# GraphSAGE sampling and aggregation on one Trainium2 core: merging the third part beside the second's decode, closing the first counts behind sort stages, counting on VectorE, key transfers from GpSimd, quarter broadcasts

## The chip, the core and the metric

One core of one Trainium2 chip runs the whole program. The metric is device microseconds of one execution; the number that counts is the median of three runs. The core's engines run side by side, each through its own queue of instructions in order: TensorE (PE, with its weight loads PEld), VectorE (DVE), ScalarE (ACT), GpSimd (POOL) and SyncE (SP). They wait for each other, and for transfers, by semaphores. SyncE, ScalarE and GpSimd issue transfers. Here semaphores named DMAHW count transfers that SyncE or ScalarE issued, those named DMASW the transfers of GpSimd; there are eight of each and they are used in turn.

## The reference, cut to what matters

```python
N, deg, D = 12500, 64, 64
E = N * deg                                   # 800,000 edges, src and dst drawn at random
nsum = _segment_sum(x[src], dst, N)           # for every edge: nsum[dst] += x[src]
h_neigh = nsum * deg_inv[:, None]
return x @ w_self + h_neigh @ w_neigh
```

## The kernel before

**Sort.** Every edge becomes one key that holds a bucket number and the two indices inside it: `dst` is cut in 87 blocks of 144, `src` in 98 blocks of 128, so there are 87 x 98 = 8,526 buckets of about 94 edges. 128 rows of 6,250 keys are sorted side by side, by stages of VectorE that take the minimum and maximum at a distance (`sort_runs`, L220). The last 30 stages (APART) are cut in portions, low columns first, so that the low part of the rows is final before the high part.

**Parts.** The buckets fall in three parts, numbered 0 to 2 in the code and called part 1, 2 and 3 in the text: 32, 20 and 16 buckets in each of 128 rows. For each part, `find_rows` counts on ScalarE, row by row, where each of its 128 stretches begins (L448, 128 counts); `st` (L451, VectorE), a transpose (TensorE) and `ix` (L455, VectorE) make indices of the counts; `gather_runs` lets GpSimd gather 128 runs by them (L463, one indirect transfer each, with one small memset as a pause behind it, or two behind the first 32 of part 1). `merge_runs` merges the 128 sorted runs on VectorE pair by pair (L276, L288), in groups (GROUPS) that are merged as their runs arrive. Then `find_buckets` or `find_and_gather` counts in windows of the merged rows where each bucket begins (L608), `store_rows` writes the rows to memory, `gather_window` gathers each bucket (L627), and `decode_buckets` splits the keys into the source and the destination index inside the bucket: `split` on VectorE (L677, L679), `narrow` on ScalarE (L684 to L690; the source indices go to memory as `sl`), `turn` on TensorE and ScalarE (L696, L697; the destination indices stay in SBUF as `dlT`). What lies beyond a bucket's place goes through `leftovers`: a list `top` is written to memory (`tops`), read back as `many`, reduced by VectorE (`ltop`, L741), written again (`lt`) and read again (`lk`). In the kernel before ScalarE issues these four transfers.

**The tile phase.** Eight buckets make a tile; there are 1,069. For 28 buckets (a chunk, 3.5 tiles) SyncE broadcasts the `sl` rows to all partitions (`slb`, L796, three buffers), and VectorE makes one-hot matrices from them (`ohs`, L798) and from `dlT` (`ohd`, L801). A tile then is 8 matmuls that pick the source rows (`ct`, L826), one eviction by ScalarE (`xg`, L836) and 16 matmuls that add them to the destinations (`acc`, L880). VectorE builds one-hots 44 buckets ahead.

**What sets the order.** From `after_sort` on the order is written by hand. `sums_and_merge` runs a loop over the tiles and places the other work between them. Part 1 is merged and decoded before the loop. In the loop, `change` goes through part 2 and then part 3: the merges first, at a rate of PACE nanoseconds of estimated VectorE time a tile, then the search and gather of buckets, then the decode. The gathers of part 3's runs are placed at one for two tiles, all in GpSimd's queue, where they wait for no tile. Once `self.changed` is set, VectorE takes a share of the evictions (L834).

Replaying the loop gives the tiles at which the work stands before: merges of part 2 to tile 247, its search and decode to 327, merges of part 3 to 656, its search and decode to 727, then 342 tiles with nothing beside them.

Of the kernel before, what the change touches and what calls it, by code (L numbers as in the profile page):

```python
# [40 lines left out]
GROUPS = ((32, 32, 32, 32), (64, 32, 32), (128,))  # L41
FIRST = 96
FROM_TILE = (0, 60, 0)
PACE = (0, 500, 420)
# [80 lines left out]
NC1 = len(WIN.w1)  # L125


def constants():
# [5 lines left out]
    for p in range(NP):  # L134
# [3 lines left out]
        first = np.array([lo + n / 2 + 0.25 for lo, n in WIN.w2[p]])  # L138
# [121 lines left out]
def merge_round(nc, src, oth, off, rstride, nruns, ln, lout, late):  # L260
# [6 lines left out]
    def at(t, first, n, step=1):  # L267
        return view(t, off + first, [[2 * ln, n2], [step, n]])
# [63 lines left out]
class Kernel:  # L332
# [136 lines left out]
    def merge_runs(self, part, u, pong):  # L469
# [8 lines left out]
        def round_(level, off, rstride, nruns):  # L478
            src = bufs[par[level]]
            args = nc, src, bufs[1 - par[level]], off, rstride  # L480
            if part == 0 and level == 6:
                def done(rows):
                    self.rows, self.lower = rows, True
                yield from merge_last(*args, lens[level], lens[level + 1], LOWER, done)
            else:
                yield from merge_round(*args, nruns, lens[level], lens[level + 1], lambda: self.late)
# [3 lines left out]
        for n in GROUPS[part]:  # L490
            level, rs, nr = 0, lens[0], n
            while nr > 1:
                yield from round_(level, first * lens[0], rs, nr)
                rs, nr, level = 2 * lens[level], nr // 2, level + 1
# [4 lines left out]
            while len(done) > 1 and done[-1][0] == done[-2][0]:  # L499
                (level, f1), (_, f0) = done.pop(), done.pop()  # L500
                yield from round_(level, f0 * lens[0], (f1 - f0) * lens[0], 2)
                done.append((level + 1, f0))
        self.rows = bufs[par[-1]]

    def store_rows(self, part, queue):
        queue.dma_start(self.d2[part][:, SIDE:SIDE + LROW[part]], self.rows[:, :LROW[part]])
# [92 lines left out]
    def junk(self):  # L599
        return self.keep.tile([128, max([512] + [n for ws in WIN.w2 for _, n in ws])], BF, name="junk2")  # L600

    def count_below(self, part, k, acc):
# [4 lines left out]
        w = view(self.rows, lo, [[1, n]])  # L607
        nc.scalar.activation(self.junk()[:, :n], w, AF.Sign, bias=c2[:, 2, k:k + 1], accum_out=acc[:, k:k + 1])  # L608

    def find_buckets(self, part):  # L610
# [4 lines left out]
        nc.sync.dma_start(self.d2[part][:, SIDE:SIDE + LOWER], self.rows[:, :LOWER])  # L615
        for k in range(KPRS[part]):
            if k == NLOWER:
                nc.sync.dma_start(self.d2[part][:, SIDE + LOWER:SIDE + LROW[part]], self.rows[:, LOWER:LROW[part]])
# [23 lines left out]
    def find_and_gather(self, part, vp):  # L642
# [6 lines left out]
        ix = self.keep.tile([128, kpr], U32, name=f"ix2_{part}")  # L649
        for k in range(kpr + LAG):  # L650
            if k == 1:
                self.store_rows(part, nc.scalar)
            if k < kpr:
                self.count_below(part, k, acc)
            if k >= LAG:
                g = k - LAG
                nc.scalar.activation(ix[:, g:g + 1], acc[:, g:g + 1], AF.Relu, scale=-0.5, bias=self.c2[part][:, 3, g:g + 1])  # L657
# [3 lines left out]
    def decode_buckets(self, part, v, vp, mps):  # L661
# [10 lines left out]
        def split(k, n, vk, _):  # L672
            w = vp.tile([128, 4, 128], I32, name="w", bufs=4 if part else 2)[:, :n]
# [8 lines left out]
        def narrow(k, n, vk, w):  # L682
            c = c0 + k // 4
            nc.scalar.activation(self.junk()[:, :n * 128], w.rearrange("p k s -> p (k s)"), AF.Sign, bias=self.edge[:, :1], accum_out=self.cnt[:, c:c + 1])  # L684
            l16 = vp.tile([128, 4, 128], BF, name="l16", bufs=4)
# [3 lines left out]
            l16 = vp.tile([128, 4, 128], BF, name="l16", bufs=4)  # L689
# [16 lines left out]
        e = self.rows if part else vp.tile([128, kpr * 2 * EXT], F32, name="e")  # L706
# [36 lines left out]
    def leftovers(self, part):  # L743
# [5 lines left out]
        nc.scalar.dma_start(self.tops[part], self.top.rearrange("p j i -> p (j i)"))  # L749
# [484 lines left out]
```

## Time and profile before

| | us |
|---|---|
| median of 3 runs (lowest, highest) | 2102.41 (2098.67, 2104.05) |
| the profiled execution's own time | 2093.24 |
| its span in the profile | 2091.5 |
| busy in the span: DVE, ACT, PE, POOL | 1869.5, 1440.1, 1060.4, 822.5 |
| sort, counts, part 1 up to the first tile | 0 to 911.8 |
| tile phase | 911.8 to 2076 |

The profile is one execution. Busy time is a mean over stages with different limits, so the stage tables are read first: for each stretch of time the busy microseconds of each engine. In the groups, a row reads: line, engine, operation, output and inputs with their shape, count, busy microseconds, mean nanoseconds of one, idle time of the engine ahead of them and what ended it. In the waits, a row reads: who waited for whom, microseconds in total, times, the longest. In the timeline, a row reads: start, duration, engine, line, operation. In the chain, a row reads: start, duration, what.

### The profile page before, as it was taken

The numbers are of one execution on the slowest core, as the hardware profiler recorded it, in microseconds if no ns is written. First come the engines' busy times: TensorE is split into PE (matmuls) and PEld (weight loads), VectorE is DVE, ScalarE is ACT, GpSimd is POOL, SyncE is SP. The second block draws the span as 40 slices with busy tenths as digits, with TensorE's granted clock in tenths as the row PEclk, the third lists the DMA queues.
The fourth block names the chain that finished last, engine by engine and source line by source line (L and its number), as shares of the span: only waits on it lengthen the run. The fifth ranks groups of instructions, "written<-read, shape, count | busy, mean of one in ns | idle before, by whom it ended". The sixth has DMA issues, their size and how long they took to land.

```text
span 2091.5 us, 60398 instructions
## 1 busy us (share of the span) xinstructions
PE 1060.4 (51%) x26074; PEld 913.7 (44%) x26074; DVE 1869.5 (89%) x2127; ACT 1440.1 (69%) x2455; POOL 822.5 (39%) x1003
## 2 busy tenths in 40 slices
PE   0060000000000000048888877889989878989987
PEld 0050000000000000047777766777877767878876
DVE  8999999299999998999999957999999858888985
ACT  7470005707884005358889999999989998888986
POOL 1000000198889850999999955101020131101101
PEclk9999999999999999998999999899999999999998
DMA  4271000001100000256677786677687867868874
GB/s 152 51 162 23 0 5 12 18 13 58 20 19 12 14 10 33 67 198 238 241 241 249 245 280 221 214 266 261 246 270 254 298 220 236 290 252 288 276 287 133
DMA packets 126816, 333.17 MB, mean 159 GB/s; under 512 B 70996, under 2 KB 82508, under 8 KB 126284
## 3 DMA queue, kind: packets, MB, share of 16 engines
q1 hardware_dynamic: 90212, 306.28, 41.0%
q0 software_dynamic: 32032, 20.73, 7.1%
q8 instruction: 205, 3.36, 0.6%
q10 hardware_dynamic: 4296, 2.22, 0.4%
q14 instruction: 71, 0.58, 0.1%
HBM read 306.31 MB, written 22.85 MB: 157 GB/s over the span
## 4 chain that ended last, share of the span: by engine, by line
DVE 47%; PE 22%; ACT 13%; issue 9%; POOL 6%; DMA 2%; ACTq 0%; DVEq 0%; SPq 0%; POOLq 0%
DVE u L288 15%; PE ct L826 13%; PE acc L880 8%; DVE b L220 7%; DVE ohd L801 6%; DVE a L220 6%; DVE ohs L798 5%; ACT xg L836 5%; POOL u L463 5%; DVE u L276 3%; ACT junka L448 2%; ACT junk L608 2%; DVE u L320 1%; ACT u L272 1%; DMA slb<-sl 1%
## 5 line engine op out<-in xcount | busy, mean ns | idle before, releaser
L836 ACT ACTIVATE xg<-ct 128x1024 f16<-128x1024 f32 x1017 | 968.5, 1101 | 90.1 <-PE ct L826 70.1
L463 POOL DMA_INDIRECT u<-d,ix x384 | 512.2, 1334 | 424.3 <-ACT junka L448 360.6
L826 PE MATMUL ct<-xh,ohs 128*128 128x128 f16 x8526 | 622.7, 226 | 73.9 <-ACT xg L836 37.9
L826 PEld LDWEIGHTS <-ohs 128*128 128x128 f16 x8526 | 515.9, 101 | 123.6 <-issue 55.3
L288 DVE TENSOR_TENSOR u<-u 128x496 f32<-128x496 f32 (+46 forms) x664 | 491.2, 772 | 24.3 <-ACT u L272 15.0
L880 PE MATMUL acc<-ohd,xg 64*128 64x72 f16 x17052 | 424.1, 197 | 82.5 <-ACT xg L836 51.4
L798 DVE TENSOR_SCALAR ohs<-slb,pidx 128x3584 f16<-128x3584 bf16 x305 | 352.9, 1157 | 69.9 <-PE ct L826 64.4
L880 PEld LDWEIGHTS <-xg 64*128 64x128 f16 x17052 | 334.8, 96 | 162.9 <-ACT xg L836 61.4
L801 DVE TENSOR_TENSOR ohd<-iota,dlT 128x2016 f16<-128x2016 bf16 x305 | 365.7, 1199 | 0.0
L453 PE MATMUL stp<-idf,st 128*128 128x128 f32 x3 | 1.4, 465 | 504.2 <-DVE st L451 504.2
L952 POOL DMA_DIRECT2D out<-o x26 | 45.1, 1755 | 538.2 <-ACT o L946 521.1
L448 ACT ACTIVATE junka<-b,c 128x220 bf16<-128x220 f32 (+43 forms) x384 | 171.2, 446 | 100.4 <-DVE b L220 89.3
L453 PEld LDWEIGHTS stp<-idf,st 128*128 128x128 f32 x3 | 0.5, 182 | 505.1 <-DVE st L451 256.5
L220 DVE TENSOR_TENSOR b<-a 128x918 f32<-128x918 f32 (+50 forms) x184 | 214.7, 1214 | 4.8 <-ACT a L222 0.3
L220 DVE TENSOR_TENSOR a<-b 128x918 f32<-128x918 f32 (+47 forms) x170 | 198.3, 1210 | 4.5 <-ACT b L222 2.0
L272 ACT ACTIVATE u<-u 128x512 f32<-128x512 f32 (+15 forms) x129 | 56.6, 504 | 156.0 <-DVE u L276 155.9
L627 POOL DMA_INDIRECT v<-d,ix x68 | 87.6, 1289 | 162.5 <-ACT ix L657 81.4
L696 PE MATMUL tr<-idb,l 128*128 128x128 bf16 x68 | 8.4, 261 | 233.5 <-ACT l L690 233.5
L222 ACT ACTIVATE a<-b 128x1 f32<-128x1 f32 (+44 forms) x57 | 23.4, 426 | 137.6 <-DVE b L220 134.6
L696 PEld LDWEIGHTS <-l 128*128 128x128 bf16 x68 | 4.8, 113 | 236.2 <-ACT l L690 235.7
L378 POOL MEMSET pad<- 128x89 f32 x448 | 103.2, 230 | 2.0
L834 DVE CAST xg<-ct 128x1024 f16<-128x1024 f32 x52 | 63.5, 1223 | 43.8 <-PE ct L826 40.0
(130 smaller groups left out, 831.2 us busy)
## 6 DMA issues: line engine op xcount, KB each, us to landing
slb<-sl SPq DMA_DIRECT2D x305, 896.0 KB
u<-d,ix POOLq DMA_INDIRECT x384
xt<-xh SPq DMA_DIRECT2D x1, 3136.0 KB
own<-os SPq DMA_DIRECT2D x12, 256.0 KB
out<-os SPq DMA_DIRECT2D x12, 256.0 KB
out<-o POOLq DMA_DIRECT2D x24, 126.0 KB
rd<-dst SPq DMA_DIRECT2D x4, 521.0 KB
rs<-src SPq DMA_DIRECT2D x4, 521.0 KB
```

What stands on the lines that cost most here:

```text
L220: nc.vector.tensor_tensor(view(dst, lo + sh, [[st, g], [1, l]]), x, y, op=op)
L272: nc.scalar.activation(at(src, a, e - a), at(oth, a, e - a), AF.Copy)
L288: nc.vector.tensor_tensor(to, at(cur, ln + lo, n), at(cur, lo + k, n), op=op)
L378: self.nc.gpsimd.memset(self.pad, 0.0)
L448: nc.scalar.activation(junk[:, :n], w, AF.Sign, bias=self.c1[:, 0, c:c + 1], accum_out=a)
L463: nc.gpsimd.indirect_dma_start(out=u[:nr, p * w:(p + 1) * w], out_offset=None, in_=src, in_offset=bass.IndirectOffsetOnAxis(ap=self.start[ ...
L627: self.nc.gpsimd.indirect_dma_start(out=self.v[:, k].bitcast(F32), out_offset=None, in_=flat(self.d2[part], 128 * PITCH2[part]), in_offset ...
L798: nc.vector.tensor_scalar(s.rearrange("p c s -> p (c s)"), b, self.pidx[:, :1], None, op0=OP.is_equal)
L801: nc.vector.tensor_tensor(d, self.iota[:, None].to_broadcast([128, 14, HN, 2]), ix, op=OP.is_equal)
L826: nc.tensor.matmul(ct[:, i * 128:(i + 1) * 128], cols[i][0], self.xh[:, (b0 + i) % NB].rearrange("p a f -> p (a f)"), start=True, stop=True)
L836: nc.scalar.activation(xg[:, :cnt * 128], ct[:, :cnt * 128], AF.Copy)
L880: nc.tensor.matmul(acc[h][:, db % OCT * HN:(db % OCT + 1) * HN], xg[r, i * 128:(i + 1) * 128], d[r], start=db % OCT == 0 and sb == 0, stop ...
```

## The change

**First counts (part 1).** The 64 counts that were left behind the first portion of the sort are placed among the first 24 stages of the second portion (BEFORE = 24); `st`, the transpose, `ix` and the gathers come behind its 25th stage; five stages and the last portion follow.

```diff
-            for _ in rows:
-                pass
...
-            for _ in self.gather_runs(0, u0):
-                pass
-            for step in portions[1]:
+            for i, step in enumerate(portions[1]):
                 step()
+                while i < BEFORE and next(rows) + 1 < EARLY + (128 - EARLY) * (i + 1) // BEFORE:
+                    pass
+                if i == BEFORE:
+                    for _ in rows:
+                        pass
+                    rows = None
+                    for _ in self.gather_runs(0, u0):
+                        pass
```

On VectorE, where `a` and `b` are the two sort buffers, `st_930`/`ix_934` and `st_992`/`ix_996` are part 1's in the kernel before and in the changed one. Before:

```order
L220 TENSOR_TENSOR b<-a 128x797 x2
L451 TENSOR_TENSOR st_930<-c_116,acc_741 128x128
L455 SCALAR_TENSOR_TENSOR ix_934<-stp,prow_117 128x128
L220 TENSOR_TENSOR a<-b 128x18x53 x2
L220 TENSOR_TENSOR b<-a 128x23x41 x2
```

After:

```order
L223 TENSOR_TENSOR a<-b 128x306x3 x2
L454 TENSOR_TENSOR st_992<-c_116,acc_741 128x128
L458 SCALAR_TENSOR_TENSOR ix_996<-stp,prow_117 128x128
L223 TENSOR_TENSOR b<-a 128x459x2 x2
L223 TENSOR_TENSOR a<-b 128x459x2 x2
```

`st` moved from behind the first portion's last stage (797 pairs) to behind the second portion's 25th.

**Third part beside the second's decode.** `change` no longer holds the merges. Two strands run in the loop: `merge` (parts 2 and 3, at PACE 450 a tile, where it was 500 and 420) and `chain` (search, gather and decode of a part that is merged). Part 3's merges begin when part 2's end; its 128 runs are merged in two groups of 64, each begun when its gathers have been placed 8 tiles before. The second merge buffer of part 3 is half as large, `w` and `l16` have two buffers in place of four, and `self.changed` is set where part 3's merges end, not its decode.

```diff
-GROUPS = ((32, 32, 32, 32), (64, 32, 32), (128,))
+GROUPS = ((32, 32, 32, 32), (64, 32, 32), (64, 64))
-FROM_TILE = (0, 60, 0)
-PACE = (0, 500, 420)
+FROM_TILE = 50
+BEFORE = 24
+PACE = 450
...
+            if chain:
+                if last != "gather" or not n % 2 and self.picked < n - 1:
+                    last = next(chain, None)
...
+            t += PACE
+            while t > 0 and merge:
+                if merging == 1 and n < FROM_TILE and self.grouped[1] >= FIRST:
+                    t = 0
+                elif merging == 2 and self.grouped[2] < 128 and (
+                        len(gathered) < self.grouped[2] + 64 or n < gathered[self.grouped[2] + 63] + 8):
+                    t = 0
+                else:
+                    dt = next(merge, None)
```

Replaying the changed loop: merges of part 2 to tile 270, its search and decode from 270 to 356, merges of part 3 from 270 to 616, its search and decode to 684, then 385 tiles.

**Later counts by VectorE.** For parts 2 and 3, `count_below` becomes one VectorE instruction that compares and sums; the constants hold the window's start in place of its middle, and the index is made on ScalarE without the factor -0.5.

```diff
+        if part:
+            nc.vector.tensor_scalar(junk[:, :n], w, c2[:, 1, k:k + 1], None, op0=OP.is_lt, op1=OP.add,
+                                    accum_out=acc[:, k:k + 1])
+        else:
+            nc.scalar.activation(self.junk[:, :n], w, AF.Sign, bias=c2[:, 2, k:k + 1], accum_out=acc[:, k:k + 1])
```

On VectorE, while part 2 is searched and decoded (`u` and `u_2108` are part 3's two merge buffers in the changed kernel, `acc_1` part 2's counts). Before, at the start of part 2's decode:

```order
L801 TENSOR_TENSOR ohd<-iota,dlT 128x2016
L708 MEMSET top_12088 128x72
L677 SCALAR_TENSOR_TENSOR w<-v,c_1_75 128x4x64 x2
L679 TENSOR_SCALAR v<-v 128x4x128
L798 TENSOR_SCALAR ohs<-slb,pidx 128x3584
```

After, in the search:

```order
L617 TENSOR_SCALAR w,acc_1_11717<-u,c_1_75 128x349
L291 TENSOR_TENSOR u<-u_2108 128x32x26
L617 TENSOR_SCALAR w,acc_1_11717<-u,c_1_75 128x366
L812 TENSOR_SCALAR ohs<-slb,pidx 128x3584
L815 TENSOR_TENSOR ohd<-iota,dlT 128x2016
```

and, further on VectorE, at the start of the decode:

```order
L812 TENSOR_SCALAR ohs<-slb,pidx 128x3584
L815 TENSOR_TENSOR ohd<-iota,dlT 128x2016
L291 TENSOR_TENSOR u_2108<-u 128x16x46
L721 MEMSET top_13355 128x72
L690 SCALAR_TENSOR_TENSOR w<-v,c_1_75 128x4x64 x2
L692 TENSOR_SCALAR v<-v 128x4x128
L291 TENSOR_TENSOR u_2108<-u 128x16x45
```

Between the one-hots there now stand counts and merges of part 3, where there was only the decode.

**Key transfers by GpSimd.** `store_rows` of parts 2 and 3 and the four transfers of `leftovers` are issued by GpSimd.

```diff
-                self.store_rows(part, nc.scalar)
+                self.store_rows(part, nc.gpsimd)
...
-        nc.scalar.dma_start(self.tops[part], self.top.rearrange("p j i -> p (j i)"))
+        nc.gpsimd.dma_start(self.tops[part], self.top.rearrange("p j i -> p (j i)"))
```

Part 1's leftovers, at the first tiles. Before, on ScalarE:

```order
L836 ACTIVATE xg<-ct 128x1024 x3
L749 DMA tops_65<-top_2596 128x72
L836 ACTIVATE xg<-ct 128x1024 x3
L753 DMA many<-tops_65 8x16x72
L836 ACTIVATE xg<-ct 128x1024 x3
```

After, on GpSimd (`u` holds part 2's runs, `u_2108` part 3's):

```order
L466 DMA u<-d_1_61,ix_1624 128x40
L381 MEMSET pad 128x89
L466 DMA u_2108<-d_2_62,ix_2101 128x36
L381 MEMSET pad 128x89
L762 DMA tops_65<-top_2564 128x72
L466 DMA u_2108<-d_2_62,ix_2101 128x36
L381 MEMSET pad 128x89
L766 DMA many<-tops_65 8x16x72
L466 DMA u_2108<-d_2_62,ix_2101 128x36
```

They moved from between ScalarE's evictions to behind GpSimd's gathers of part 2's last runs. VectorE's reader of `many` stands at the same tile as before.

**Quarter broadcasts.** Each chunk of `sl` comes in four transfers, to every fourth partition each, from SyncE in a row.

```diff
-            nc.sync.dma_start(b, bass.AP(tensor=src.tensor, offset=src.offset, ap=[[0, 128], [1, 28 * 128]]))
+            for j in range(4):
+                nc.sync.dma_start(b[j::4], bass.AP(tensor=src.tensor, offset=src.offset, ap=[[0, 32], [1, 28 * 128]]))
```

In SyncE's queue a transfer waits for the one eight places before it. Before, that is eight chunks back (and three buffers bind first); in the changed kernel it is the same quarter two chunks back.

More of the change, by code (lines that the diff above doesn't have):

```diff
@@ L125 @@
 NC1 = len(WIN.w1)
+JUNK = max(n + n % 2 for _, n in WIN.w2[0])
 def constants():
@@ L1152, in sums_and_merge @@
         gathers = self.gather_runs(2, u2)
-        change = None
-        part = 0
+        gathered = []
+        chain = None
+        part, merging = 0, 1
+        work, second = ExitStack(), ExitStack()
         last = None
@@ L1179, in sums_and_merge @@
[L1179 to L1190 removed]
+            if chain is None and part + 1 < merging:
+                part += 1
+                assert self.rows[part] is (u1, u2)[part - 1]
+                if part == 2:
+                    second.close()
+                vp = work.enter_context(tc.tile_pool(name=f"v{part}", bufs=1))
+                chain = self.change(part, vp, mps)
+                last = None
@@ L1200, in sums_and_merge @@
+        assert merging == 3 and part == 2 and not chain
         runs.close()
```

144 lines of the change are left out of this document (67 added, 77 removed).

## The prediction

> **What bounds the kernel now.** I read the page first, then the busy time by stage, then who waited for whom in each stage, then the timeline at three places.
>
> ```profile
> span 2091.5 us, 60398 instructions
> DVE 47%; PE 22%; ACT 13%; issue 9%; POOL 6%; DMA 2%; ACTq 0%; DVEq 0%; SPq 0%; POOLq 0%
> ```
>
> VectorE (DVE) carries half of the chain that ended last, but a mean over the span hides who is the limit where. The stages (columns: stretch, length, busy us and instructions of PE, PE's weight loads, DVE, ACT, POOL, then TensorE's granted clock and the DMA share) say it:
>
> ```profile
> 369.30:407.40 38.10, 0.00 (x0) 0.00 (x0) 0.01 (x1) 36.05 (x128) 0.00 (x0) 1.00 0.05 22
> 911.80:1197.00 285.20, 239.67 (x5907) 207.62 (x5905) 279.58 (x390) 245.57 (x302) 261.41 (x274) 0.91 0.73 245
> 1197.00:1302.00 105.00, 84.54 (x2012) 70.83 (x2012) 69.34 (x82) 103.05 (x178) 60.91 (x59) 0.95 0.76 248
> 1302.00:1649.00 347.00, 312.07 (x7967) 269.64 (x7965) 344.54 (x338) 326.21 (x389) 40.90 (x19) 0.96 0.75 253
> 1649.00:1742.00 93.00, 72.20 (x1718) 60.45 (x1717) 60.76 (x74) 88.11 (x148) 27.30 (x25) 0.94 0.74 246
> 1742.00:2076.00 334.00, 304.14 (x8231) 266.90 (x8228) 286.44 (x299) 283.22 (x326) 32.95 (x21) 0.98 0.77 265
> ```
>
> The first row is a hole: VectorE does nothing for 38.1 us while ScalarE (ACT) counts. The other five cut the tile phase (1,069 tiles of 24 matmuls) where the order of instructions changes job: tiles 0 to 247 with part 2's merges, 247 to 327 with part 2's search and decode, 327 to 656 with part 3's merges, 656 to 727 with its decode, then 342 bare tiles. Where merges run, VectorE is full (98% and 99%); in the two decode stages ScalarE is (98% and 95%) and VectorE has 35.7 and 32.2 us free; in the last, TensorE (91%) is nearest to its limit, at 334/342 = 0.977 us a tile.
>
> **A. The first counts.** Removed: the hole.
>
> ```profile
> DVE st L451 <- ACT junka L448: 40.3, 3, 38.1
> 463.34 1.12 DVE L220 TENSOR_TENSOR b<-a 128x918 f32<-128x918 f32 x1
> 409.54 1.05 POOL L463 DMA_INDIRECT u<-d,ix  x1 [360.63 <-ACT junka L448]
> L463 POOL DMA_INDIRECT u<-d,ix x23 | 36.3, 1579 | 3.5 <-issue 3.4
> L463 POOL DMA_INDIRECT u<-d,ix x28 | 31.0, 1107 | 4.4 <-issue 4.4
> 512.58 2.73 DMA u<-d,ix
> 515.10 1.43 DVE L220 TENSOR_TENSOR b<-a 128x574 f32<-128x574 f32 x2
> ```
>
> `st` now stands 25 sort stages later. Those took from 408.5 to 463.3, 54.8 us; begun at 369.3 they end at 424.1, and ScalarE's 64 counts (36.05 us busy in the hole) are done by then, so `st` waits for nothing. VectorE saves 38.1 us, but GpSimd (POOL) starts its gathers at 426.2, not 409.5. Before, the first merge began at 516.4 straight behind the sort; now VectorE is ready at 516.4 - 38.1 = 478.3, and needs the 32nd gather. While the wide sort stages run (426 to 476, the x23 row) a gather with its pauses takes 50/23 = 2.17 us; behind them (476 to 516, x28) 40/28 = 1.43, and 1.63 with the second pause that the first 32 have. Now 4 fall in wide stages and 27 behind: 426.2 + 4 x 2.17 + 27 x 1.63 = 478.9, landed 2.73 later at 481.6. New wait 3.3 us, net **-34.8**. If every gather took 2.17 the wait were 18 and the gain 20; the ends are -20 and -38. Later groups' gathers have ten and more us in hand.
>
> **B. Key transfers by GpSimd.** For ScalarE this removes some 14 issues, nothing on the path. But GpSimd works its queue in order, and before tile 0 it holds 32 gathers of part 1's windows and 32 of part 2's runs.
>
> ```profile
> 923.06 1.26 ACTq L753 DMA_DIRECT2D many<-tops  x1
> 930.98 1.38 POOL L463 DMA_INDIRECT u<-d,ix  x1 [0.16 <-issue]
> 931.46 3.02 DVE L741 MAX8 ltop<-many 8x8 f32<-8x73 f32 x16
> 932.71 0.94 POOL L463 DMA_INDIRECT u<-d,ix  x1 [0.16 <-issue]
> 934.00 0.95 POOL L463 DMA_INDIRECT u<-d,ix  x1 [0.16 <-issue]
> 934.51 0.28 DVE L757 TENSOR_SCALAR_CACHE_REDUCE many<-ltop 8x128 f32<-8x128 f32 x1
> 935.30 8.61 POOL L463 DMA_INDIRECT u<-d,ix  x1 [0.16 <-issue]
> 953.78 1.44 POOL L463 DMA_INDIRECT u<-d,ix  x1 [0.16 <-issue]
> ```
>
> `many` was issued by ScalarE at 923.06 and read by VectorE at 931.46 without a wait. At that time GpSimd starts the 23rd of part 2's last 32 gathers (930.98); the 32nd starts at 953.78. In the changed queue `tops` and `many` stand behind that and behind one and two of part 3's. So VectorE comes to `ltop` at 931.5 - 34.8 - 0.6 (one merge fewer ahead of it) = 896 and must wait for 11 gathers, `tops` and its landing (part 3's second gather fits beside), `many` and its landing, with its merges and one-hots queued behind. With VectorE quiet a gather and its pause take 1.29 us (932.71 to 934.00): 11 x 1.29 + 2 x 2.73 + 0.6 = 20 us: **+20**. At the pace of 930.98 to 953.78, 2.5 us each with the long one, it is 33; with half of the gathers already gone, 10. VectorE is the limit in this stage, so all of it counts. The 1.29 pace fits best, since the 8.61 us gather began between ScalarE's two last such issues, which now wait in GpSimd's own queue. The same steps for parts 2 and 3 meet a GpSimd that is busy 40.9 of 347 us and cost nothing. Part 2's row store queues behind part 3's last gathers, which end about when merge 2 does (261 of 285 us busy to 1197); the decode reads it 48 tiles later, which covers some 20 us.
>
> [...]
>
> **C. Part 3's merges beside part 2's decode; later counts on VectorE.** By the order merge 2 now ends at tile 270 (PACE 450 for 500), part 2 is searched and decoded in 270 to 356, merge 3 runs from 270 to 616, part 3 is searched and decoded in 616 to 684. Where VectorE is the limit I add its work.
>
> ```profile
> L801 DVE TENSOR_TENSOR ohd<-iota,dlT 128x2016 f16<-128x2016 bf16 x93 | 111.5, 1199 | 0.0
> L798 DVE TENSOR_SCALAR ohs<-slb,pidx 128x3584 f16<-128x3584 bf16 x93 | 107.0, 1151 | 0.0
> L288 DVE TENSOR_TENSOR u<-u 128x912 f32<-128x912 f32 x2 | 2.2, 1102 | 0.0
> L288 DVE TENSOR_TENSOR u<-u 128x1792 f32<-128x1792 f32 x3 | 6.1, 2018 | 0.0
> L677 DVE SCALAR_TENSOR_TENSOR w<-v,c 128x256 int32<-128x256 int32 x10 | 3.7, 412 | 0.0
> L608 ACT ACTIVATE junk<-u,c 128x99 bf16<-128x99 f32 (+19 forms) x20 | 15.1, 756 | 1.5 <-DVE u L288 1.5
> ```
>
> - A tile of one-hots: two instructions for 3.5 tiles, each overlapping the next by some 0.06 to 0.09 us (515.10 + 1.43 ends after the merge's start at 516.44): 2.23/3.5 = 0.64 us.
> - A merge: from 912 and 1792 elements 1.04 ns an element and 0.15 us fixed, 0.09 of it beyond the overlap. Part 3's elements stay the same, but two groups of 64 make 94 more instructions: 8.5 us.
> - 20 counts of 7,077 elements. The nearest row reduces 128 elements in 0.28 us, just the merges' price, so 7.4 + 20 x 0.16 = 10.6; at half a cycle an element 7, at twice 18.
> - Part 2's decode: 3.7 us of splits and some 6.7 of smaller ones, 10.4. ScalarE has 8 tiles or so of this at 1.5 us: 4 more. With two `l16` buffers for four its narrowing waits for the store of four tiles before, 4.5 us back; a landing of 2.73 fits in that, so 0.
>
> Tile phase starts at 911.8 - 34.8 = 877.0. To tile 270: 285.2 + 23 x 0.64 + 20 = 320, 1197. To 616: the 347.0 of merge 3 with 329 tiles + 17 x 0.64 + 8.5 + 10.6 + 10.4 + 4 = 391, 1588. To 684: before, 93.0 for 71 tiles; 68 are 89, less 16 counts off ScalarE at about 0.75 (12 us) and some 8 that VectorE now evicts, since it helps from the merges' end: 69, 1657.
>
> **D. Quarter broadcasts.** 385 bare tiles at 0.977 are 376, to 2033.
>
> ```profile
> PE acc L880 <- issue: 14.3, 12, 3.6
> PE ct L826 <- issue: 8.3, 7, 2.0
> q8 instruction: 205, 3.36, 0.6%
> L796 SPq DMA_DIRECT2D slb<-sl x305: 319/319/428, 904.5 to 2060.1; - x153
> 1177.84 6.31 DMA slb<-sl
> 1520.25 6.25 DMA slb<-sl
> ```
>
> In the last stage TensorE stands 22.6 us in 19 gaps that wait for no semaphore. An instruction fetch brings 3.36 MB/205 = 16.4 kB, 60398/205 = 295 instructions, some six tiles; a late fetch is my reading of the gaps, and no row pairs them. Fetches go through the same DMA engines as the broadcasts of 896 kB, which fill 77% of their time. If a quarter lets a fetch in after a fourth of the time, most gaps of up to 2 us close: 22.6 x 385/342 = 25, of which I take 70%: **-18**; ends 0 and -25. In the VectorE-bound stages such gaps are covered. SP issues 1,220 times instead of 305: 4 x 0.32 = 1.3 us a chunk, inside its 3.5 x 0.977 = 3.42 us. VectorE's three more waits a chunk run ahead of a 1.2 us instruction.
>
> [...]
>
> **Sum.** 2033 - 18 = 2015, and 15.5 behind the last tile: 2030.5 against 2091.5, -61.0. The profiled execution took 2093.24, 9.2 below the median of 2102.41; I take the 61 off the median: **2041**.
>
> **Rivals.**
> - Fetch gaps stay: the same without the 18, 2060. For it: no row shows the pairing.
> - ScalarE binds in 270 to 356, where it keeps evictions, index writes and narrowing: 103 of 105 us busy before. At 1.3 us a tile instead of 1.13, 86 tiles cost 15: 2056. Against: 15 us of counts leave it.
> - `ltop` waits the full 33: 2054.
> - Slower: SP now waits, ahead of each quarter, for the quarter two chunks back (before: eight transfers back). Two chunks in flight bear 3.42 us a chunk only if one lands in 6.84; 6.25 and 6.31 us stand close, with no queueing of four pieces in them. Should it land in 8, a chunk takes 4.0, a tile 1.14, and 385 bare tiles lose 0.21 each, 81: 2122. It decides from about 7.3 us.
>
> **Chances.** Forecast 0.48; gaps stay 0.16; ScalarE 0.12; full wait 0.08; two chunks in flight 0.11, slower; a milder form of it that eats the gain, 0.05. A measurement here can tell 0.3%, 6 us. So faster 0.84, same 0.05, slower 0.11. Low end: hole fully gained (3), wait of 10 (10), gaps all closed (7), 13 from the middle stages being bound by VectorE alone with cheap counts: 2008. High end: gaps stay and ScalarE or the full wait binds, 2075, and 15 for A's other end: 2090.
>
> **What would show it.** A: no wait of `st`, the first merge near 482. B: VectorE idle ahead of `ltop` by 10 to 33 us, ended by a GpSimd transfer. C: no hole in VectorE from tile 270 to 616, some 391 us. D: TensorE's "issue" gaps under 8 us in the bare tiles, below 0.95 us a tile. Wrong if SP waits longest for its own transfers.

## The result, and the profile after

Median of four runs 2074.2 us (2069.7 to 2079.2); before 2100.5 on the same chip, ratio 0.9875 (0.9844 to 0.9905): 26 us faster where 61 were forecast. One execution of a kernel below (part 3 merged in two groups) ran slow, 2120.6 us, and is left out of that kernel's median and ratio. The profiled execution took 2069.70 us. Its page, span and chain:

```profile
span 2068.0 us, 61827 instructions
DVE 46%; PE 16%; POOL 13%; DMA 10%; issue 9%; ACT 3%; SPq 3%; DVEq 0%; POOLq 0%; ACTq 0%
DMA slb<-sl 10%; DVE u L291 9%; DVE b L223 9%; PE ct L840 9%; POOL u L466 9%; DVE a L223 8%; DVE ohs L812 7%; PE acc L894 6%; DVE ohd L815 6%; SPq L810 3%; POOL pad L381 2%; DVE u L279 2%; POOL v L639 2%; DVE u L323 1%; ACT xg L850 1%
```

VectorE still leads; GpSimd (POOL, mostly its gathers) has 13% of the chain where it had 6%, and the broadcasts 10% where they had 1%. The stages, with the columns of the table of before: the former hole, then tiles 0 to 270, 270 to 616, 616 to 684, 684 to the end.

```profile
369.30:407.40 38.10, 0.00 (x0) 0.00 (x0) 37.51 (x36) 36.12 (x126) 0.00 (x0) 0.50 0.05 19
883.60:1202.00 318.40, 263.86 (x6482) 228.03 (x6481) 293.90 (x405) 268.23 (x331) 268.14 (x306) 0.90 0.77 238
1202.00:1602.00 400.00, 343.38 (x8419) 295.23 (x8418) 395.96 (x517) 361.64 (x470) 62.59 (x48) 0.92 0.79 243
1602.00:1683.00 81.00, 65.70 (x1642) 57.22 (x1635) 74.20 (x108) 67.12 (x97) 29.92 (x26) 0.92 0.82 268
1683.00:2056.00 373.00, 343.53 (x9331) 301.13 (x9327) 323.26 (x334) 321.83 (x374) 46.62 (x29) 0.99 0.86 269
```

The hole is filled (37.51 of 38.10). Two waits of VectorE are new, in the timeline: the first merge behind the sort, and `ltop`.

```profile
482.33 2.09 DVE L279 TENSOR_TENSOR u<-u 128x896 f32<-128x896 f32 x2 [4.98 <-POOL pad L381]
920.12 2.98 DVE L754 MAX8 ltop<-many 8x8 f32<-8x73 f32 x16 [17.23 <-DMA many<-tops]
902.94 0.95 POOL L466 DMA_INDIRECT u<-d,ix  x1 [0.16 <-issue]
904.24 0.96 POOL L466 DMA_INDIRECT u<-d,ix  x1 [0.16 <-issue]
...
914.39 0.59 POOL L762 DMA_DIRECT2D tops<-top  x1
```

While VectorE waits, GpSimd works off its gathers at 1.3 us each (902.94 to 904.24) until `tops` is issued at 914.39.

VectorE's costliest groups, first three of before, then four of after:

```profile
L288 DVE TENSOR_TENSOR u<-u 128x496 f32<-128x496 f32 (+46 forms) x664 | 491.2, 772 | 24.3 <-ACT u L272 15.0
L276 DVE TENSOR_TENSOR u<-u 128x896 f32<-128x896 f32 (+23 forms) x94 | 87.2, 956 | 1.1
L834 DVE CAST xg<-ct 128x1024 f16<-128x1024 f32 x52 | 63.5, 1223 | 43.8 <-PE ct L826 40.0 <-ACT o L946 2.0 <-ACT xg L836 1.8
```

```profile
L291 DVE TENSOR_TENSOR u<-u 128x544 f32<-128x544 f32 (+42 forms) x746 | 503.2, 703 | 28.7 <-ACT u L275 17.4
L279 DVE TENSOR_TENSOR u<-u 128x896 f32<-128x896 f32 (+19 forms) x106 | 88.6, 864 | 6.2 <-POOL pad L381 5.0
L848 DVE CAST xg<-ct 128x1024 f16<-128x1024 f32 x67 | 81.7, 1221 | 44.3 <-PE ct L840 34.6 <-ACT xg L850 7.2 <-ACT o L960 2.1
L617 DVE TENSOR_SCALAR_CACHE_REDUCE w<-u,c 128x99 bf16<-128x99 f32 (+34 forms) x36 | 21.7, 604 | 0.1
```

The change gave VectorE 13.4 us more of merges (591.8 against 578.4), 18.2 of evictions and 21.7 of counts: 53 us (its busy time in all grew by 47.5, from 1869.5 to 1917.0; instructions of different groups overlap a little, so the parts add up to more). This added work is the key to part C below.

### The profile page after: what moved, and what is told of

It is laid out like the page before. It is cut to its first block, busy times and chain, and to the rows that moved or that the text cites. A ratio compares the mean times of both kernels' runs of the same rounds, so it can differ in the third digit from the quotient of the medians.

```text
span 2068.0 us, 61827 instructions
## 1 busy us (share of the span) xinstructions
PE 1059.4 (51%) x26074; PEld 915.7 (44%) x26074; DVE 1917.0 (93%) x2309; ACT 1413.9 (68%) x2383; POOL 807.6 (39%) x1017
## 3 DMA queue, kind: packets, MB, share of 16 engines
q1 hardware_dynamic: 104852, 306.34, 45.4%
## 4 chain that ended last, share of the span: by engine, by line
DVE 46%; PE 16%; POOL 13%; DMA 10%; issue 9%; ACT 3%; SPq 3%; DVEq 0%; POOLq 0%; ACTq 0%
DMA slb<-sl 10%; DVE u L291 9%; DVE b L223 9%; PE ct L840 9%; POOL u L466 9%; DVE a L223 8%; DVE ohs L812 7%; PE acc L894 6%; DVE ohd L815 6%; SPq L810 3%; POOL pad L381 2%; DVE u L279 2%; POOL v L639 2%; DVE u L323 1%; ACT xg L850 1%
## 5 line engine op out<-in xcount | busy, mean ns | idle before, releaser
L850 ACT ACTIVATE xg<-ct 128x1024 f16<-128x1024 f32 x1002 | 945.5, 1068 | 106.5 <-PE ct L840 93.9
L466 POOL DMA_INDIRECT u<-d,ix x384 | 495.7, 1291 | 439.6 <-DVE ix L458 376.1
L291 DVE TENSOR_TENSOR u<-u 128x544 f32<-128x544 f32 (+42 forms) x746 | 503.2, 703 | 28.7 <-ACT u L275 17.4
L223 DVE TENSOR_TENSOR b<-a 128x918 f32<-128x918 f32 (+50 forms) x184 | 214.8, 1214 | 4.5
L275 ACT ACTIVATE u<-u 128x128 f32<-128x128 f32 (+13 forms) x145 | 58.7, 470 | 181.9 <-DVE u L279 181.0
L848 DVE CAST xg<-ct 128x1024 f16<-128x1024 f32 x67 | 81.7, 1221 | 44.3 <-PE ct L840 34.6
```

The costliest lines, as they stand in the source:

```text
L223: nc.vector.tensor_tensor(view(dst, lo + sh, [[st, g], [1, l]]), x, y, op=op)
L291: nc.vector.tensor_tensor(to, at(cur, ln + lo, n), at(cur, lo + k, n), op=op)
L466: nc.gpsimd.indirect_dma_start(out=u[:nr, p * w:(p + 1) * w], out_offset=None, in_=src, in_offset=bass.IndirectOffsetOnAxis(ap=self.start[ ...
L848: nc.vector.tensor_copy(xg[:, :cnt * 128], ct[:, :cnt * 128])
L850: nc.scalar.activation(xg[:, :cnt * 128], ct[:, :cnt * 128], AF.Copy)
```

## The experiments

Ratios are to the kernel before, run between them on the same chip; microseconds from a difference of ratios are at 2100.

| kernel | median us | ratio (95%) |
|---|---|---|
| the changed kernel | 2074.2 | 0.9875 (0.9844, 0.9905) |
| changed, whole broadcasts | 2084.9 | 0.9912 (0.9886, 0.9938) |
| changed, leftovers on ScalarE | 2064.5 | 0.9812 (0.9789, 0.9835) |
| the same once more | 2061.1 | 0.9809 (0.9774, 0.9844) |
| changed, leftovers on ScalarE, whole broadcasts | 2070.6 | 0.9848 (0.9826, 0.9870) |
| changed, leftovers and later counts on ScalarE | 2064.6 | 0.9850 (0.9835, 0.9865) |
| changed, leftovers on ScalarE, evictions later | 2058.1 | 0.9823 (0.9808, 0.9838) |
| changed, leftovers on ScalarE, quarters to neighbours | 2289.5 | 1.0909 (1.0869, 1.0949) |
| before + first counts | 2070.0 | 0.9842 (0.9815, 0.9869) |
| before + first counts + quarters | 2058.5 | 0.9827 (0.9810, 0.9845) |
| before + first counts + quarters + later counts on VectorE | 2037.1 | 0.9693 (0.9665, 0.9721) |
| the same, 18 stages for the first counts | 2029.0 | 0.9662 (0.9634, 0.9690) |
| the same once more | 2032.3 | 0.9667 (0.9637, 0.9697) |
| that, part 3 merged in two groups | 2046.8 | 0.9743 (0.9710, 0.9777) |
| that, two buffers of `w` and `l16` | 2028.2 | 0.9657 (0.9627, 0.9687) |

### The first counts alone

The kernel before with the edit of the first counts, word for word as in the change.

> The kernel before with the first counts alone moved (BEFORE = 24). The changed kernel starts its tile phase 28.2 us sooner than the kernel before. Theory: that is all from this part, so 28 us less than before, 2072, ratio 0.9866. Rival: the gathers, which start 17 us later on GpSimd, hold something further on that the changed kernel hides behind its ltop wait (part 3's gathers into merge 3, the first windows): 10 to 20 us less, ratio 0.990 to 0.995.

0.9842, 33 us: more than the whole change's 26. The theory holds. By these ratios the rest of the change together cost 7 us, though the two intervals overlap; the error is to be looked for there. The first tile's eviction came at 878.6 here and at 883.6 in the changed kernel, so 5 us of the rest are lost before the tiles. They go in part 1's merges: in each of its four groups VectorE waits about 0.8 us for a copy by ScalarE (L275) for which it does not wait here, and runs the merges behind it 0.3 us longer. No run tests which piece of the change does that.

### Leftovers on ScalarE, and whole broadcasts

```diff
-        nc.gpsimd.dma_start(self.tops[part], ...)
+        nc.scalar.dma_start(self.tops[part], ...)
... the same for many, lt and lk
-            for j in range(4):
-                nc.sync.dma_start(b[j::4], ... [[0, 32], [1, 28 * 128]]))
+            nc.sync.dma_start(b, ... [[0, 128], [1, 28 * 128]]))
```

> The changed kernel with each chunk broadcast in one transfer again. Three theories of the quarters. Nil: they neither brought the 18 us of the prediction nor cost anything, since TensorE's issue gaps stay (22.1 us in the changed kernel's bare tiles, 22.6 before): 2074, as the changed kernel. Cost: SP's four issues of a median 0.59 us (0.32 for the whole one), VectorE's 15.5 us of idle time ahead of the one-hots and packets of 335 ns for 300 slow the tile phase: 2050 to 2065, SP waits some 250 us for VectorE in the bare tiles again and VectorE hardly for a landing. Gain: the quarters did help and something else lost time in the bare tiles: 2082 to 2095, more than 25 us of issue gaps.

> The changed kernel with the four transfers of the leftovers issued by ScalarE again, in all three parts; row stores stay with GpSimd. Theory: VectorE's 17.2 us ahead of ltop are the price of the place in GpSimd's queue alone; then they go whole, and the end comes 15 to 18 us sooner: 2056 to 2059, with a wait of under 2 us ahead of ltop. Rival: the place would be slow all the same, because GpSimd's gathers (two of 4.4 and 8.6 us before) or the first broadcasts hold the tiles there: under 6 us gained, 2068 to 2074.

> Both of the two edits: whole broadcasts and leftovers issued by ScalarE. If the two costs lie in different stages, the gains of the two kernels beside it add up: with 17 for the leftovers, 2057 by nil, 2035 to 2048 by cost of the quarters, 2065 to 2078 by gain. If they overlap at the first tiles (the first chunks' landing and the wait of ltop are both at tiles 0 to 25), 5 us or more of the sum is missing.

> The changed kernel with the leftovers' transfers on ScalarE once more, beside these three, as their anchor: ratio 0.979 to 0.984 as before if the ratios of two sessions can be compared to 0.3%.

The wait of `ltop` goes with the place of the transfers: 0.9875 to 0.9812 with quarters, 0.9912 to 0.9848 with whole broadcasts, 13 us both times, where 15 to 18 were expected; the second run of it on another chip gave 0.9809. The quarters gain: 0.9912 to 0.9875, and 0.9848 to 0.9812, 8 us both times; neither "nil" nor "cost" holds; "gain" does, at half of the prediction's 18. The two add up. What the quarters do stands in TensorE's waits over the same 339 tiles (727 to 1066), whole broadcasts first, then quarters:

```profile
PE acc L893 <- issue: 21.3, 13, 4.1
PE ct L839 <- issue: 9.5, 11, 1.8
```

```profile
PE acc L894 <- issue: 12.4, 14, 2.6
PE ct L840 <- issue: 4.9, 7, 1.2
```

With gaps over 0.3 us counted, the issue gaps are 22.3, 30.1, 33.3 and 27.6 us in the four profiles with whole broadcasts (mean 28.3; the 22.3 is that of the kernel before, from which I forecast), and 14.1 to 23.8 in ten with strided quarters (mean 18.1; the kernel with two groups, whose merges end later, and the three profiles whose first tiles took longer, further below, are left out). The tiles take 335.9 and 326.6 us in the mean. So it is the gaps that shrink, by a third. The packet records now pair them with fetches: in the changed kernel each of 22 gaps from tile 684 on ends 1.2 to 1.6 us after one of the 72 fetch packets of 16 kB there has ended; in all fourteen profiles every one of these gaps ends 1.2 to 1.7 us after such a packet. SP pays in issue time. Its transfers (ns: shortest, median, longest), and its waits in these tiles with whole broadcasts and with quarters:

```profile
L810 SPq DMA_DIRECT2D slb<-sl x1220: 447/592/1979, 875.2 to 2043.1; - x175
```

```profile
SPq L809 <- DVE ohs L811: 277.0, 93, 8.0
```

```profile
SPq L810 <- DVE ohs L812: 46.1, 43, 3.7
```

A quarter takes 592 ns to issue, where the whole took 319: SP, which waited 277 us for a free buffer, now waits 46. It is nearer to its own limit, but not at it: 46 us of such waits are left in 321.4.

The transfer itself gets slower: from a chunk's first issue to the end of its last packet it is 5.8 us in the median in the bare tiles, 4.4 to 4.8 with whole broadcasts. The kernel gains 8 us all the same, with issue gaps that are 10 us shorter (28.3 to 18.1 in the mean). How a fetch gets through sooner is not shown; the fetch packets take 0.6% of the engines' time on both pages.

### Half the broadcasts

```diff
+            if c % 56 == 0:
                 b = pool.tile([128, 28 * 128], BF, name="slb", bufs=3)
                 ...
                 nc.sync.dma_start(b, ...)
```

> The kernel before, in which every second chunk is not loaded: its one-hots are made from the chunk before (the sums are of other edges), so the broadcasts move half the bytes. Theory of the prediction, a late instruction fetch waits for broadcast packets: TensorE's issue gaps over the last 339 tiles, 22 to 33 us with whole broadcasts, fall under 10 us, and these tiles take 320 us or less (331 before). Rival, the fetch is late by itself: gaps stay at 18 us or more, each opening 1.2 to 1.6 us after a fetch packet ended, and the tiles at 325 to 335 us.

```profile
PE acc L882 <- issue: 8.0, 6, 3.7
PE ct L828 <- issue: 6.0, 5, 2.2
```

This kernel leaves out every second broadcast, so its sums are of other edges. It ran once (2080.3 us), with 14.0 us of gaps and 321.3 us for the tiles: between the two theories. Half the traffic takes the gaps to about half (28.3 in the mean, 22.6 in the kernel before itself) and does not end them. The broadcasts are a part of the cause, as far as one execution shows it; some gaps are left with half the traffic.

### Quarters to neighbouring partitions

```diff
-                nc.sync.dma_start(b[j::4], ...)
+                nc.sync.dma_start(b[32 * j:32 * j + 32], ...)
```

> The changed kernel with the leftovers' transfers on ScalarE, each quarter going to 32 neighbouring partitions in place of every fourth one. If the quarter's long issue (0.59 us in the median for 0.32) and its longer packets (335 ns for 300) come from the stride, both fall back here, SP has time again, and the tiles may gain: issue 0.32 to 0.40, 2055 to 2062. If they come from the number of transfers in flight or their size, issues stay at 0.55 or more and the time within 4 us of the kernel with the stride. If neighbouring partitions share a path into SBUF, packets get longer still (over 380 ns) and it is slower, 2070 or more.

The third case, and far beyond its price: 230 us. The broadcasts' queue (packets, MB, share of 16 engines), in the kernel that this one starts from (changed, leftovers on ScalarE) and here, then TensorE's waits in tiles 727 to 1066 and SP's issues:

```profile
q1 hardware_dynamic: 104852, 306.34, 46.1%
```

```profile
q1 hardware_dynamic: 104852, 306.34, 59.2%
PE acc L894 <- issue: 54.7, 29, 4.2
PE ct L840 <- issue: 34.8, 14, 4.7
L810 SPq DMA_DIRECT2D slb<-sl x1220: 302/419/2122, 876.5 to 2251.4; - x175
```

The same bytes keep the engines busy for 59.2% of 2284.6, 1352 us, instead of 46.1% of 2062.8, 951; the issue gaps are 90 us, and each of the 43 longer than 0.3 us ends 1.3 to 1.8 us after a fetch packet. An issue takes 419 ns in the median without the stride and 592 with it, so part of the long issue goes with the stride; packets and fetches suffer without it. The run comes out as the third case does, in the time and in the packets (over all 104,852 of the queue 206 ns each in the mean, by the 1352 us of 16 engines, where the 951 give 145; the 380 was meant for the broadcasts' own alone); a path into SBUF that neighbouring partitions share shows in no row.

### Counts back on ScalarE, evictions later

Both on the changed kernel with leftovers on ScalarE. The first puts `count_below` back as it was; the second:

```diff
                     else:
-                        self.changed = True
...
                         lefts[part] = [self.leftovers(part), 0]
+                        self.changed = part == NP - 1
```

> The changed kernel with the leftovers' transfers on ScalarE, and now the later counts on ScalarE too. The 36 counts are 24.6 us on VectorE, which was busy 396 of 400 us in tiles 270 to 616. Theory, VectorE binds from 270 to 684: most of the 24.6 us comes back, 12 to 24 us less than the 2064 of the kernel with the leftovers alone: 2041 to 2052. Rival, both engines are full in the decode stages (ScalarE gets 36 counts of about 1 us with their readout): what VectorE saves ScalarE spends, 2060 to 2070. Second rival, ScalarE then binds alone in 270 to 356: slower, 2072 or more.

> The changed kernel with the leftovers' transfers on ScalarE, and VectorE's share of the evictions begun only when part 3's decode has ended, as in the kernel before. Theory: in tiles 616 to 684 VectorE (74 of 81 us busy, 12.2 of them 10 evictions) binds, so taking these off gives 5 to 9 us: 2055 to 2060. Rival: ScalarE takes them at the same cost (67 of 81 us busy, 10.2 more), so the stage stays at 80: 2064, within 4. Slower than 2068 would say that the help was needed.

Neither gained: 0.9850 and 0.9823 against 0.9812. With the counts on ScalarE it is 8 us more by the ratios, whose intervals touch, and the same by the medians. The stages of tiles 270 to 356 and 616 to 684, first with the counts on VectorE, then on ScalarE:

```profile
1188.00:1302.40 114.40, 87.16 (x2096) 73.86 (x2097) 113.06 (x160) 102.00 (x149) 38.48 (x30) 0.91 0.79 250
1585.10:1665.50 80.40, 65.92 (x1664) 57.25 (x1664) 75.93 (x109) 68.75 (x99) 29.33 (x25) 0.94 0.86 274
```

```profile
1186.80:1301.70 114.90, 88.89 (x2097) 75.25 (x2097) 103.65 (x120) 112.85 (x189) 37.77 (x30) 0.93 0.78 248
1584.20:1665.80 81.60, 64.61 (x1661) 55.06 (x1662) 66.33 (x77) 77.29 (x131) 30.21 (x25) 0.98 0.83 271
```

What one engine is relieved of, the other takes up: VectorE 113.06 and ScalarE 102.00 become 103.65 and 112.85, and the stage keeps its length. With merges beside the decode the engine that has the counts is busy 98 to 99% of it and the other 89 to 90%. With the evictions later, tiles 616 to 684 take 79.7 us instead of 80.4, with VectorE busy 66.7 us and ScalarE 75.4: again the work has only changed places.

### First counts and quarters; then the later counts, without the merges beside

The kernel before with first counts and quarters; then also with the changed kernel's `count_below`; then with `BEFORE = 18`.

> The kernel before with the first counts moved and quarter broadcasts, nothing else. By the pairs run so far (2084.9 against 2074.2, 2070.6 against 2064.5) the quarters bring 6 to 10 us; first counts alone gave 2070.0: so 2060 to 2064, ratio 0.979 to 0.982. If that holds, part 3's merges beside the decode and VectorE's counts together brought nothing, and this equals the 2064.5 of the changed kernel with leftovers on ScalarE. If those two did bring something that the noise hides, it comes out at 2068 or above.

> The kernel before with first counts moved, quarter broadcasts and the later counts on VectorE, but part 3's merges behind part 2's decode as before. Theory: the third part's merges beside the second's decode and the counts on VectorE both spend the same idle time of VectorE. In the kernel with first counts and quarters alone, VectorE stands idle 37.5 us in tiles 247 to 356 and 32.5 us in 656 to 727 while ScalarE is idle 9.2 and 6.4 us; the counts there cost ScalarE about 1 us each and VectorE 0.69. So counts moved alone shorten these stages by 15 to 28 us: 2031 to 2044, ratio 0.970 to 0.975. Rival: the search is a chain of waits (count, index, gather), so the stages keep their time: 2054 to 2062, ratio 0.980 to 0.984. Second rival: the counts hold back VectorE's one-hots there: slower than 2062.

> The same with the first counts closed behind 18 stages in place of 24. Theory: the 4.7 to 5.1 us for which the first merge waits for its gathers go, since GpSimd starts about 13 us sooner, and st still waits for nothing (36 us of counts in some 40 us of stages): 3 to 6 us less than the kernel beside it. Rival: ScalarE doesn't get through its counts by then, st waits 2 to 6 us, and nothing is gained, or the gathers slow down in the wide stages and the wait stays.

First counts and quarters alone give 0.9827, and the changed kernel with the leftovers on ScalarE 0.9812: what the two differ in, part C of the prediction, brought nothing that shows. Tiles 247 to 356 and 656 to 727 (search and decode), counts on ScalarE and then on VectorE:

```profile
1166.40:1309.70 143.30, 112.65 (x2690) 95.28 (x2686) 105.71 (x139) 134.18 (x214) 49.94 (x48) 0.94 0.76 235
1617.60:1712.70 95.10, 73.10 (x1776) 61.16 (x1770) 62.56 (x75) 88.81 (x149) 27.26 (x25) 0.96 0.79 246
```

```profile
1165.60:1296.00 130.40, 111.58 (x2686) 94.77 (x2681) 115.19 (x179) 122.72 (x173) 61.68 (x60) 0.94 0.81 258
1605.50:1688.40 82.90, 72.04 (x1780) 60.29 (x1777) 71.78 (x107) 78.70 (x117) 30.68 (x25) 0.98 0.90 281
```

Here ScalarE is the limit and VectorE idle (37.6 and 32.5 us), and the stages shorten by 12.9 and 12.2 us. In the time it is 0.9827 to 0.9693, 28 us by the ratios, as much as was expected at most, and 21 by the medians of the two sessions. With 18 stages the first merge no longer waits:

```profile
477.36 2.09 DVE L277 TENSOR_TENSOR u<-u 128x896 f32<-128x896 f32 x2
```

It starts at 477.36 with no wait, where it was 482.33; `st` waits for nothing. 0.9693 to 0.9662 and 0.9667 is 6 us, as expected, though the intervals overlap. This version and its variant with two buffers are the fastest: 2029 and 2032 us, 70 below the kernel before and 44 below the changed one by the ratios.

With these runs the later counts and the merges beside the decode make a table of four (quarters and first counts in all, leftovers on ScalarE; the right column has all that came with the merges beside the decode: two groups, smaller buffers, evictions by VectorE from the merges' end, row stores by GpSimd):

| | merges behind the decode | merges beside it |
|---|---|---|
| counts on ScalarE | 0.9827 | 0.9850 |
| counts on VectorE | 0.9693 | 0.9812 |

Counts alone bring 28 us. Merges beside the decode bring nothing in either row; with the counts they take back 25. In tiles 0 to 727 VectorE is busy 807 us in the lower right kernel and 775 in the lower left one: some 13 of the 32 us are merges and some 18 evictions.

### What takes it back

On the fastest kernel, one piece of the changed kernel at a time:

```diff
-GROUPS = (..., (128,))
+GROUPS = (..., (64, 64))
```

```diff
-            w = vp.tile(..., bufs=4 if part else 2)
+            w = vp.tile(..., bufs=2)
... l16 likewise: two for four in parts 2 and 3
```

```diff
         assert self.rows is u
         closing()
+        self.changed = part == NP - 1
```

> The kernel with first counts (18 stages), quarters and counts on VectorE, part 3's merges behind part 2's decode, with part 3's runs merged in two groups of 64 in place of one of 128: 94 more merge instructions. They cost 13.8 us of VectorE's busy time in the changed kernel. Theory: VectorE is full where part 3 is merged (idle 0.7 of 270 us in tiles 356 to 616), so all of it is paid: 12 to 16 us more, 2041 to 2045, ratio 0.972 to 0.974. Rival: the smaller pieces fit into what is idle elsewhere: within 4 us of 2029.

> The same kernel with one group of 128, but with two buffers of w and of l16 in place of four in the decodes of parts 2 and 3, as the changed kernel has. Theory: ScalarE waits for the store of the chunk before, 3.9 us in part 3's decode of the changed kernel, in a stage in which it is the limit: 3 to 8 us more, 2032 to 2037. Rival, the prediction's: nothing, within 3 us of 2029.

> The same kernel with VectorE's share of the evictions begun where part 3's merges end, as the changed kernel has it, in place of where its decode ends. ScalarE is idle 4.6 of 83 us in tiles 656 to 727 and VectorE 12.4. Theory: VectorE takes some 10 evictions into that idle time and ScalarE loses 10 us, so half of it shows: 3 to 6 us less, 2023 to 2026. Rival: VectorE's evictions wait for TensorE and hold back its counts and one-hots (6.2 us of such waits in the changed kernel's stage): nothing gained, or up to 5 us lost.

In the profiled executions of these three the first 270 tiles, which no edit touches, took 98 to 118 us longer than in the kernel that they start from. The medians were 2156.7, 2141.7 and 2154.2 us (one of the 18 executions took 2083.7), so their times say nothing of the edits; the cause is open. In the rows of one of them ScalarE stands 14.16 us with nothing to wait for:

```profile
927.18 1.02 ACT L843 ACTIVATE xg<-ct 128x1024 f16<-128x1024 f32 x1 [14.16 <-issue]
```

The evictions were not run again. In that run tiles 270 to 800 took 580 us against 568 and 571 in the two runs without the edit, which speaks against a gain, no more. The other two were, beside the kernel that they start from:

> The kernel with first counts (18 stages), quarters and counts on VectorE once more, beside its two variants. The three variants run before it took some 90 to 110 us longer over tiles 0 to 270, which their edits do not touch. If that came with those runs alone, this one gives 2025 to 2036 again; if it belongs to this kernel under some condition that was not there the first time, it gives 2120 or more, with the time lost in tiles 0 to 270.

> Two groups of 64 for part 3, beside the kernel with one group. Theory: VectorE is full where part 3 is merged, the 94 more instructions (13.8 us) are paid whole: 12 to 16 us more than the kernel beside it. Rival: within 4 us. In the first run tiles 270 to 800 took 594.7 us against 567.9, which speaks for 14 or more.

> Two buffers of w and l16 for four, beside the kernel with four. Theory: ScalarE's waits for the store, some 4 us in each decode, show: 3 to 8 us more. Rival, the prediction's: nothing, within 3 us. In the first run tiles 270 to 800 took 575.1 us against 567.9.

Two groups cost about 15 us (2046.8 us against 2032.3 beside it; 0.9743 against 0.9667), two buffers nothing (0.9657). Tiles 356 to 656, part 3's merges, with one group and with two:

```profile
1294.90:1602.70 307.80, 281.74 (x7253) 240.89 (x7253) 307.20 (x280) 293.42 (x352) 41.76 (x18) 0.98 0.84 260
```

```profile
1286.30:1604.00 317.70, 289.77 (x7261) 249.82 (x7262) 313.24 (x366) 297.56 (x369) 32.29 (x18) 0.95 0.83 256
```

86 instructions more and 10 us in this stage, of which VectorE is busy for 6 and idle for 4; the merges then end some 30 tiles later. Over all tiles they cost VectorE 11.2 us more. If the groups cost as much beside the decode, where no run tests it, 15 of the 25 us are their price. The change took them together with the half second merge buffer; no run has the whole buffer beside the decode. The other 10 are not split further.

## Why the prediction was right and wrong

**A, first counts: right.** -34.8 forecast, 33 measured alone. The first merge came at 482.33 (481.6 forecast), after a wait of 4.98 (3.3; by the forecast's own rows five gathers at 2.17 us, not four, end before the wide stages do, which gives 482.1).

**B, transfers by GpSimd: right, a little large.** +20 forecast; the trace shows 17.23 ended by `many`, with gathers at 1.3 us, as argued; taken away, it gives 13 by the ratios, whose intervals reach past 17, and tiles 0 to 270 take 303.2 us instead of 319.2. VectorE came to `ltop` at 902.9, not 896.

**C: wrong, and most of the miss.** -28 forecast (what remains of the 61); measured as the difference between the kernels with and without it, +1 with whole broadcasts (0.9842 to 0.9848), -3 with quarters (0.9827 to 0.9812), with the row stores' move to GpSimd and the 5 us before the first tile in it. The step that failed is "To 684: ... 69": I took 12 us of counts and 8 of evictions off ScalarE and did not add them to VectorE's own sum, as I had done for part 2. The stage took 81.0, with VectorE busy 74.20, more than the 69 forecast for the whole; and with the counts or the evictions given back to ScalarE it took 81.6 and 79.7 (80.4 in the kernel beside these). The step "To 616: ... 391" was 9 short (400.00): merges at 0.09 us for each added instruction, where the rows give 13.4/94 = 0.14, and part 2's counts at 10.6, measured 13.0 with their readouts. Tile 270 came at 1202 where 1197 was forecast, which is the 5 us lost in part 1's merges. By its stages the profiled execution ended 37 us late (2068.0 for 2030.5): 5 at tile 270, 9 to 616, 12 to 684, 15 in the bare tiles, and 4 gained behind them.

The thought behind both steps was that idle time of VectorE would be filled, and it was. In tiles 0 to 727 of the kernel with first counts and quarters alone it is 77.6 us: 37.6 and 32.5 in the two stages shown, 7.0 and 0.6 in the other two (length less DVE busy):

```profile
879.40:1166.40 287.00, 242.82 (x5915) 209.73 (x5915) 280.05 (x391) 245.98 (x302) 256.91 (x283) 0.91 0.80 243
1309.70:1617.60 307.90, 283.39 (x7264) 242.28 (x7262) 307.35 (x280) 293.98 (x353) 41.84 (x18) 0.97 0.84 260
```

With all of C and the leftovers on ScalarE it is 25.1 in the same tiles: 1.3 and 4.5 in the two stages shown, and here 8.8, 2.3 and 8.2.

```profile
884.80:1188.00 303.20, 263.95 (x6495) 226.95 (x6495) 294.44 (x405) 268.58 (x332) 270.67 (x302) 0.93 0.82 250
1302.40:1585.10 282.70, 252.29 (x6284) 217.05 (x6281) 280.39 (x357) 257.29 (x319) 21.84 (x14) 0.93 0.79 242
1665.50:1716.80 51.30, 44.45 (x1042) 38.16 (x1041) 43.12 (x72) 37.61 (x48) 7.52 (x5) 0.87 0.79 226
```

52 us were filled, and VectorE's work in these tiles had grown by 51 us (755.7 to 806.9): 25 of counts, 18 of evictions and 13 of merge instructions of the change's own making, which overlap in part. The tiles took 832 us, as before (833). What the counts earn alone was spent again, some 15 us of it on the two groups.

**D, quarters: right cause, twice the size.** -18 forecast, 8 measured. "I take 70%" of the gaps failed: a third closed, and the bare tiles took 0.97 us each, not under 0.95. The bare tiles' 0.977 was the best of four profiles with whole broadcasts (0.977 to 1.004), so the stage came 15 late although the quarters gained.

**Rivals.** "Fetch gaps stay" was half true (17.9 us of 22.6 in the last 339 tiles). Two chunks in flight: VectorE waited 13.0 us in all for broadcasts (5.1 before); a chunk lands 5.8 us after its first issue in the median and 7.3 in one of twenty, where 7.3 was to decide. "ScalarE binds in 270 to 356": the pace was the one named (114 us for 86 tiles, 1.33), but the fuller engine was VectorE, 113.06 of 114.40, with ScalarE at 102.00; only with the counts on ScalarE was it ScalarE (112.85 of 114.90). The full wait of 33 did not come. The time, 2074, lies in the upper half of the range (2008 to 2090).

## What to carry to other kernels

Idle time of an engine can be spent once: when two parts of a change both mean to use it, add all the work of both on that engine, stage by stage, before counting either. Here the counts earned 28 us alone, and beside the merges 8 by the ratios and none by the medians. And the stage whose two engines were busy 94% of the time between them gained nothing from moving work from one to the other.

## What the runs showed of the hardware

- The broadcasts to 32 neighbouring partitions kept the DMA engines busy 1.4 times as long as those to every fourth partition (1352 against 951 us for 306 MB), and TensorE's issue gaps were 90 us in 339 tiles, where they were 18 in the mean. Each gap over 0.3 us ended 1.2 to 1.8 us after a fetch packet. How the place where a broadcast lands acts on a fetch was not shown.
- On SP a transfer of a quarter of the bytes to every fourth partition took longer to issue (592 ns in the median) than the whole one (319); to neighbouring partitions it took 419.
- TensorE's granted clock was 0.50 from 369 to 880 us, ahead of the tiles, in the profiled run of the changed kernel and 1.00 in that of the kernel before, and VectorE's sort stages (1214 ns each in the mean, both times) and ScalarE's counts (446 and 448 ns) did not move.
